# An attention and ELU-MLP kernel on one core: six-token runs for q and k of two batches, casting transfers for v, and reciprocals and batch 0 spread over other engines

## The chip, the cores and the metric

The kernel runs on one core of one Trainium2 chip. The core has five engines with instruction streams of their own: TensorE (PE in the profile, with its weight loads PEld), VectorE (DVE), ScalarE (ACT), GpSimd (POOL) and SyncE (SP), and 16 DMA engines that move data between the device's memory and the core's SBUF. Times are device microseconds of one execution; a kernel's time is the median of several.

## The reference, cut to what matters

```python
batch, n_heads, seq, head_dim = (8, 8, 576, 64)          # q, k, v in float32
# global part: q, k, v averaged over groups of 4 tokens, 144 of them, full softmax attention,
# each row of the result repeated 4 times
out_up = np.repeat(sm_attn(q_d, k_d, v_d), 4, axis=2)
# local part: softmax attention over |i - j| < 4
mask = np.abs(pos[:, None] - pos[None, :]) < 4
scores = np.where(mask, scale * np.matmul(q, k.transpose(0, 1, 3, 2)), -1000000000.0)
...
attn_out = out_up + out_local
# then a two-layer MLP on the 4608 tokens, 512 wide, 2048 hidden
x = attn_out.transpose(0, 2, 1, 3).reshape(4608, 512)
h = x @ w_in
g = np.where(h > 0.0, h, np.exp(np.minimum(h, 0.0)) - 1.0)
return g @ w_out
```

## The kernel before, in words

All matmuls run on fp16 operands; inputs and output are fp32.

**Attention.** The work goes by batch b (8 of them) and by pair j of heads (4 per batch). For each pair, `load` brings q, k and v as 96 tokens by (2 heads, 6 blocks, 64) into slots named `ld`. For most batches a token's row of 64 values is one run of 256 B. For the batches in `PAIRED` (0 and 1) q and k come as runs of two tokens, 512 B (L355). v comes with three tokens on either side of each block, the halos, which are transfers of their own of 3 partitions each (L366, L372, L375). All these are issued on SP's queue. `cast` turns them to fp16 (`c16`, `v16`): on DVE for q and k of batch 0, else on POOL (L409). `transposes` multiplies each block by an identity with averaging columns beside it, which gives the transposed q or k and its average over 4 tokens at once (L434 for paired batches, L440 for the others); ACT copies the results out of PSUM (L453, L462, L464). The averages of v come from another small matmul and a copy on DVE (L474, L483). `scores` does the local scores (96 queries by 102 keys) and the global ones (L499, L507), then two exps on ACT (L516) and a multiplication by the band's mask on DVE (L524).

**Denominators.** Once per batch, 76 small matmuls sum all exps (L544), and DVE takes reciprocals (L567). For batches 0 and 1 (`BY_PE`) PE spreads them over 128 partitions (L581), and ACT and DVE, in turn, copy them to `rcb` (L591). For the other batches they go to device memory (L596, rd<-rc) and come back in two broadcasting transfers (L602, rcb<-rd), all on ACT's queue.

**Outputs.** Per pair, PE computes local and global outputs (L626, L634), DVE multiplies by the reciprocals (L643, `xn`), and POOL adds local and global parts into the 512-token tiles `xt` of the MLP (L655).

**MLP.** Nine tiles of 512 tokens. mm1: 16 groups of 4 matmuls 128x512 against WI (L672), then exp on ACT (L678) and two operations on DVE (L680, L683) into `gt`. mm2: 4 groups of 16 matmuls against WO (L695), a copy on ACT (L710), a store on SP's queue (L713). WI and WO are cast while they are transferred, four transfers each, issued by POOL (L395).

**What sets the order.** A planner (`class Plan`) holds every operation with an engine, an assumed duration, a rank and the buffers it needs. It simulates all engines: each takes, whenever it is free, the ready operation of lowest rank whose buffers it can get. Transfers are modelled as one stream, with a rate in bytes per us for each kind and a depth beyond which SP issues no more. The order that comes out is emitted, and each engine then runs its own list strictly in that order. `PARAM` sets the ranks (how far attention of batch b leads tile b), `SLOTS` the buffers of each kind. `GATES` says which operation each of the eight weight transfers waits for, as (batch, pair, index of the cast). PSUM has eight banks; an attention operation takes two neighbouring banks or one, and shares them with the MLP.

Of the kernel before, what the change touches and what calls it, by code (L numbers as in the profile page):

```python
# [28 lines left out]
PAIRED = (0, 1)  # L29
BY_PE = (0, 1)  # L30
GATES = ((0, 2, 2), (0, 3, 0), (0, 3, 2), (0, 3, 2), (1, 1, 2), (1, 2, 2), (1, 3, 2), (1, 3, 2))


def _np_consts():
# [10 lines left out]
    by2 = np.zeros((QB, 48), dtype=np.float16)  # L45
    by2[np.arange(QB), np.arange(QB) // 2] = 0.25
    one = np.concatenate([eye, by4], axis=1)
    pair = np.concatenate([by2, eye, by2, np.zeros((QB, 96), dtype=np.float16)], axis=1)
# [10 lines left out]
    return m, one, pair, vr, ind, seed, sel.reshape(128, 640)  # L59
# [22 lines left out]
class Plan:  # L82
# [8 lines left out]
    def op(self, eng, dur, rank, fn, reads=(), writes=(), after=(), name="", nbytes=0, rate=1.0):  # L91
        o = Op(eng, dur, rank, fn, name)
        o.nbytes, o.rate = nbytes, rate
        for b in list(reads) + list(writes):
            o.pre.update(b.writers)
            if b not in o.bufs:
                o.bufs.append(b)
        o.pre.update(after)
        for b in writes:
            b.writers.append(o)  # L100
        for b in o.bufs:
            b.ops.append(o)
        self.ops.append(o)
        return o

    BANKS = ("two", "one", "hp", "op")

    def _take(self, b, free):
# [5 lines left out]
        banks = free["bank"]  # L114
# [29 lines left out]
    def run(self):  # L144
        free = {k: set(range(n)) for k, n in self.slots.items()}
        free["bank"] = set(range(8))
        self.count = {"hp": 0, "op": 0}
# [21 lines left out]
        events, now, dma, order = [], 0.0, 0.0, []  # L169
        n = 0  # L170
        while n < len(self.ops):
            for e, todo in ready.items():
                if busy[e] > now + 1e-9 or not todo or (e == "SP" and dma > now + self.depth):
                    continue
                todo.sort(key=lambda o: (o.rank, o.i))
                for o in todo:
                    got = []
# [11 lines left out]
                else:  # L189
                    continue  # L190
# [5 lines left out]
                if o.nbytes:  # L196
                    dma = max(dma, now + dur) + o.nbytes / o.rate
                    done = dma + 1.9
                    if e == "SP" and dma > now + self.depth:
                        heapq.heappush(events, (dma - self.depth, -1, None))  # L200
# [8 lines left out]
            now = events[0][0]  # L209
            while events and events[0][0] <= now + 1e-9:  # L210
                _, _, o = heapq.heappop(events)
                if o is None:
                    continue
                for q in o.post:
# [10 lines left out]
    def emit(self):  # L225
        for o in self.order:
# [4 lines left out]
    "ld": 9, "c16": 4, "v16": 8, "qt": 3, "kt": 3, "ex": 8, "vd": 8,  # L231
# [3 lines left out]
PARAM = dict(M0=43.0, P=36.0, LAG=0.8, LEAD=48.6, GAP=5.3, SC=2.7, DEN=28.0, OUT=9.0, OUTG=2.3, LOAD=22.6, warm=22.0,  # L235
             DEPTH=7.3, WI=-44.0, WO=14.0, WOG=6.0)
# [3 lines left out]
def kernel(  # L240
# [15 lines left out]
    def many(kind, shape, dt=FP16):  # L256
# [3 lines left out]
        "ld": many("ld", [KW, 2, NB, 64], FP32),  # L260
        "c16": many("c16", [QB, NB, 2, 64]),
        "v16": many("v16", [KW, NB, 2, 64]),
# [28 lines left out]
    plan.warm, plan.depth = PARAM["warm"], PARAM["DEPTH"]  # L291
# [3 lines left out]
    m_np, one_np, pair_np, vr_np, ind_np, seed_np, sel_np = _np_consts()  # L295
    C, cbuf = {}, {}

    def const(a, name, rank):
        t = sb.tile(list(a.shape), FP16, tag=name, name=name)
        src = nc.inline_tensor(a, name=name + "c").ap()  # L300
        C[name] = t
        return op("SP", 0.35, rank, lambda: nc.sync.dma_start(out=t[:], in_=src), name=name,
                  nbytes=a.size * 2, rate=150e3)

    c_pair = const(pair_np, "PAIR", -50)
    c_vr = const(vr_np, "VR", -48.5)
    c_mask = const(m_np, "MASK", -46.5)
    c_ind = const(ind_np, "IND", -44.5)
    c_seed = const(seed_np, "SEED", -44.4)
    c_sel = const(sel_np, "SEL", -40.5)  # L310
    c_one = const(one_np, "ONE", -35)
# [23 lines left out]
    def twos(src, b, j):  # L335
        a = src[b, 2 * j]
        return bass.AP(
            tensor=a.tensor, offset=a.offset,
            ap=[[2 * D, QB], [S * D, 2], [192 * D, 3], [1, 2 * D]],
        )  # L340
# [3 lines left out]
    def load(b, j):  # L344
        n = NPAIR * b + j
        r = -49.9 + 2 * j if b == 0 else late(b, j) - PARAM["LOAD"]
        bufs = []
        for i, (src, kind) in enumerate(((q, "ld"), (k, "ld"), (v, "ld"))):
            x = Buf(kind)

            def go(src=src, x=x, i=i):
                t = at(x)
                if i < 2 and b in PAIRED:
                    to = t[0:QB].rearrange("p e (c j) d -> p e c (j d)", c=3)
                    nc.sync.dma_start(out=to, in_=twos(src, b, j))  # L355
                elif i < 2:
                    nc.sync.dma_start(out=t[0:QB], in_=rows(src, b, j, 0, QB, 0, NB))
                else:
                    nc.sync.dma_start(out=t[3 : 3 + QB], in_=rows(src, b, j, 0, QB, 0, NB))  # L359
                    lo = 1 if n == 0 else 0  # L360
                    hi = NB - 1 if n == NPAIR * B - 1 else NB
                    if lo:
                        nc.gpsimd.memset(t[0:3, :, 0, :], 0.0)
                    if hi < NB:
                        nc.gpsimd.memset(t[96:KW, :, NB - 1, :], 0.0)
                        nc.sync.dma_start(  # L366
                            out=t[96:99, :, NB - 1, :], in_=rows(src, b, j, 93, 3, NB - 1, 1)[:, :, 0]
                        )
                    for c0, nblk, tok, p in ((lo, NB - lo, -3, 0), (0, hi, QB, 99)):
                        to, a = t[p : p + 3, :, c0 : c0 + nblk, :], rows(src, b, j, tok, 3, c0, nblk)  # L370
                        if nblk == NB:
                            nc.sync.dma_start(out=to, in_=a)  # L372
                        else:
                            for e in range(2):
                                nc.sync.dma_start(out=to[:, e], in_=a[:, e])  # L375

            rate = 290e3 if i < 2 and b in PAIRED else 185e3
            op("SP", 0.4 if i < 2 else 1.3, r + 0.01 * i, go, writes=[x], nbytes=96 * 768 * 4, rate=rate,
               name=f"load{b}{j}{'qkv'[i]}")
            bufs.append(x)  # L380
        st[b, j] = {"ld": bufs}

    wi_ops, wo_ops = {}, {}

    def weights(i):
        wi = i < 4
        if wi:
            src = moe_w_in.rearrange("(c p) m -> p c m", p=128)[:, :, 512 * i : 512 * i + 512]
            to, r = WI[:, :, 512 * i : 512 * i + 512], PARAM["WI"] + 0.1 * i
        else:  # L390
            n = 4 * (i - 4)
            src = moe_w_out.rearrange("(c p) m -> p c m", p=128)[:, n : n + 4, :]
            to, r = WO[:, n : n + 4, :], PARAM["WO"] + PARAM["WOG"] * (i - 4)
        b, j, x = GATES[i]
        o = op("POOL", 1.3, r, lambda: nc.gpsimd.dma_start(out=to, in_=src), name=f"w{i}", after=[st[b, j]["op"][x]],  # L395
               nbytes=128 * 8192, rate=320e3)
        (wi_ops if wi else wo_ops)[i % 4] = o

    def cast(b, j):
        s, r = st[b, j], late(b, j)  # L400
        s["c"], s["op"] = [], []
        for i, x in enumerate(s["ld"]):
            y = Buf("v16" if i == 2 else "c16")
            p = KW if i == 2 else QB
            eng = "DVE" if b == 0 and i < 2 else "POOL"

            def go(x=x, y=y, p=p, eng=eng):
                f = (nc.vector if eng == "DVE" else nc.gpsimd).tensor_copy
                f(out=at(y)[:], in_=at(x)[0:p].rearrange("p e c d -> p c e d"))  # L409

            s["op"].append(
                op(eng, 0.5 if eng == "DVE" else 0.85, r - 8 + i, go, reads=[x], writes=[y], name=f"cast{b}{j}{i}")
# [6 lines left out]
    def transposes(b, j):  # L419
        s, r = st[b, j], late(b, j)  # L420
        yq, yk, yv = s["c"]
        m = b in PAIRED
# [343 lines left out]
```

## Time and profile before

| | |
|---|---|
| median of 3 runs | 397.23 us (395.22 to 397.68) |
| the profiled execution's own time | 400.66 us |
| its span, first to last instruction | 398.6 us |
| granted TensorE clock, mean | 0.982 |
| busy: PE, DVE, ACT, POOL | 355.6, 231.7, 210.4, 130.6 us |
| DMA packets | 119716, 48.12 MB |
| first MoE matmul (L672) starts | 53.16 us |
| last MoE matmul (L695) ends | 394.9 us |

PE is TensorE's matmuls; their ends are modelled and neighbours overlap, so the distance from start to start says what one costs. A line such as "L409 POOL CAST v<-ld" gives the line of the code, the engine, the operation and the buffers. "SPq" is SP's DMA queue. A time in brackets is the idle time before an instruction, and the arrow names what ended it.

### The profile page before, as it was taken

How to read it: one execution, taken by the hardware profiler on the slowest of the kernel's cores; microseconds unless marked ns; L12 is line 12 of the kernel's file. 1: busy time of each engine (PE TensorE's matmuls, PEld its weight loads, DVE VectorE, ACT ScalarE, POOL GpSimd, SP SyncE). 2: the span in 40 equal slices, each digit the busy share in tenths (PEclk: the TensorE clock that was granted, in tenths of full speed). 3: DMA queues.
4: the chain of work that ended last, by engine and by line, in shares of the span. 5: the costliest groups of instructions: out<-in, count | busy, mean ns of one | idle time of the engine just before them, and what ended most of it. 6: DMA issues, size and time to landing. Idle time of an engine off the chain costs nothing.

```text
span 398.6 us, 8777 instructions
## 1 busy us (share of the span) xinstructions
PE 355.6 (89%) x3536; PEld 191.8 (48%) x3536; DVE 231.7 (58%) x404; ACT 210.4 (53%) x353; POOL 130.6 (33%) x207
## 2 busy tenths in 40 slices
PE   3741798999998399979999999989999999999996
PEld 2531654556554245545555545544555454444442
DVE  1430648766786237754868665857676666564530
ACT  3650376565974066635765756475749334444421
POOL 1333466039703472236127603570350023000000
PEclk9999998999999789989999999999999999999999
DMA  9999999958239997956449729701300221001012
GB/s 184 199 210 170 216 172 146 197 122 185 54 73 209 196 225 148 183 104 150 116 93 196 181 87 181 132 35 53 102 27 28 68 66 53 28 26 54 27 53 79
DMA packets 119716, 48.12 MB, mean 121 GB/s; under 512 B 98359, under 2 KB 115069, under 8 KB 119677
## 3 DMA queue, kind: packets, MB, share of 16 engines
q1 hardware_dynamic: 111325, 38.74, 44.5%
q0 software_dynamic: 4224, 4.19, 6.6%
q10 hardware_dynamic: 4128, 4.65, 5.3%
q8 instruction: 27, 0.44, 0.5%
q14 instruction: 12, 0.10, 0.1%
HBM read 42.11 MB, written 9.66 MB: 130 GB/s over the span
## 4 chain that ended last, share of the span: by engine, by line
PE 75%; DMA 10%; SPq 7%; DVE 3%; issue 2%; ACT 2%; POOL 2%; ACTq 0%; POOLq 0%; DVEq 0%
PE bank L695 29%; PE bank L672 29%; DMA ld<-in_v_dram 5%; DMA rcb<-rd 4%; SPq L372 4%; PE bank L440 3%; PE bank L499 3%; PE bank L626 2%; PE bank L544 2%; PE bank L474 2%; SPq L359 2%; PE bank L434 1%; DVE e L680 1%; POOL v L409 1%; PE bank L507 1%
## 5 line engine op out<-in xcount | busy, mean ns | idle before, releaser
L672 PE MATMUL bank<-xt,WI 128*128 128x512 f16 x576 | 146.3, 384 | 3.3 <-DVE gt L683 1.8
L695 PE MATMUL bank<-WO,gt 128*128 128x512 f16 x576 | 146.5, 384 | 0.0
L678 ACT ACTIVATE e<-bank 128x512 f16<-128x512 f32 x144 | 85.8, 599 | 86.8 <-PE bank L672 69.3
L680 DVE TENSOR_SCALAR e<-e 128x512 f16<-128x512 f16 x144 | 56.4, 393 | 81.3 <-ACT e L678 80.9
L683 DVE SCALAR_TENSOR_TENSOR gt<-bank,e 128x512 f16<-128x512 f32 x144 | 98.8, 688 | 5.0
L672 PEld LDWEIGHTS <-WI 128*128 128x128 f16 x576 | 53.7, 98 | 63.6 <-issue 6.9
L695 PEld LDWEIGHTS <-gt 128*128 128x128 f16 x576 | 53.2, 99 | 57.0 <-issue 2.2
L409 POOL CAST c<-ld 96x768 f16<-96x768 f32 x56 | 48.0, 866 | 91.2 <-PE bank L440 47.2
L655 POOL TENSOR_TENSOR xt<-xn 128x288 f16<-128x288 f16 (+8 forms) x96 | 49.1, 538 | 45.4 <-DVE xn L643 45.3
L516 ACT ACTIVATE ex<-bank 102x864 f16<-102x864 f32 x64 | 55.6, 889 | 14.0 <-PE bank L507 13.8
L409 POOL CAST v<-ld 102x768 f16<-102x768 f32 x32 | 28.8, 901 | 61.4 <-DMA ld<-in_v_dram 40.3
L643 DVE TENSOR_TENSOR xn<-bank,rcb 128x720 f16<-128x720 f32 x32 | 28.3, 903 | 18.7 <-POOL xt L655 7.9
L710 ACT COPY os<-bank 128x512 f32<-128x512 f32 x36 | 21.2, 588 | 33.1 <-PE bank L695 25.4
L524 DVE TENSOR_TENSOR ex<-ex,MASK 102x1152 f16<-102x1152 f16 x32 | 28.7, 898 | 14.1 <-ACT ex L516 14.1
L474 PE MATMUL bank<-v,VR 102*72 102x128 f16 x192 | 18.5, 240 | 18.2 <-POOL v L409 16.0
L440 PE MATMUL bank<-ONE,c 96*128 96x120 f16 x288 | 22.3, 217 | 6.2 <-DVE xn L643 6.2
L440 PEld LDWEIGHTS <-c 96*128 96x128 f16 x288 | 19.1, 98 | 15.6 <-issue 6.5
L453 ACT CAST qt<-bank 128x720 f16<-128x720 f32 x24 | 18.2, 758 | 15.5 <-PE bank L440 14.8
L474 PEld LDWEIGHTS <-VR 102*72 102x72 f16 x192 | 14.9, 126 | 22.8 <-issue 15.6
L462 ACT CAST kt<-bank 128x576 f16<-128x576 f32 x32 | 22.1, 689 | 6.5 <-PE bank L440 4.9
L483 DVE CAST vd<-bank 72x256 f16<-72x256 f32 x32 | 13.2, 413 | 17.6 <-PE bank L474 17.4
L499 PEld LDWEIGHTS <-kt 64*102 64x102 f16 x384 | 13.5, 138 | 17.3 <-issue 9.6
(34 smaller groups left out, 176.3 us busy)
## 6 DMA issues: line engine op xcount, KB each, us to landing
ld<-in_q_dram SPq DMA_DIRECT2D x32, 288.0 KB
ld<-in_k_dram SPq DMA_DIRECT2D x32, 288.0 KB
ld<-in_v_dram SPq DMA_DIRECT2D x32, 288.0 KB
out_dram<-os SPq DMA_DIRECT2D x36, 256.0 KB
rcb<-rd ACTq DMA_DIRECT2D x12, 360.0 KB
WI<-in_moe_w_in_dram POOLq DMA_DIRECT2D x4, 512.0 KB, 9.8
WO<-in_moe_w_out_dram POOLq DMA_DIRECT2D x4, 512.0 KB, 6.8
ld<-in_v_dram SPq DMA_DIRECT2D x62, 9.0 KB
```

Of the source, the lines that this page charges most:

```text
L409: f(out=at(y)[:], in_=at(x)[0:p].rearrange("p e c d -> p c e d"))
L440: nc.tensor.matmul(o, t[:, c, :, :], C["ONE"][:], start=True, stop=True)
L474: nc.tensor.matmul(one(z, 0, 72, 128 * (c // 3), 128 * (c // 3) + 128), C["VR"][:, 48 - 24 * (c % 3) : 120 - 24 * (c % 3)], t[:, c, :, :], ...
L516: lambda e=e: nc.scalar.activation(out=at(x)[:, e], in_=two(sc[e], 0, KW, 0, HB + SD), func=AF.Exp, scale=SCALE),
L524: nc.vector.tensor_tensor(out=a, in0=a, in1=mk, op=AB.mult)
L643: lambda: nc.vector.tensor_tensor(out=at(w)[:], in0=two(z, 0, 128, 0, GW), in1=at(y)[:, j], op=AB.mult),
L655: nc.gpsimd.tensor_tensor(out=at(xt(t))[:, j, o : o + n - a], in0=ln, in1=gn, op=AB.add)
L672: nc.tensor.matmul(one(h, 0, 128, 0, TBLK), WI[:, dc, 128 * fc : 128 * fc + 128], at(x)[:, dc, :], start=(dc == 0), stop=(dc == DMC - 1),)
L678: op("ACT", 0.55, r, lambda: nc.scalar.activation(out=at(e)[:], in_=one(h, 0, 128, 0, TBLK), func=AF.Exp), reads=[h], writes=[e], name=f"e ...
L680: op("DVE", 0.36, r, lambda: nc.vector.tensor_scalar(out=at(e)[:], in0=at(e)[:], scalar1=1.0, scalar2=-1.0, op0=AB.min, op1=AB.add), reads ...
L683: op("DVE", 0.69, r, lambda: nc.vector.scalar_tensor_tensor(out=at(gt)[:, fc, :], in0=one(h, 0, 128, 0, TBLK), scalar=0.0, op0=AB.max, in1 ...
L695: nc.tensor.matmul(one(z, 0, 128, 0, DM), at(gt)[:, fc, 128 * tt : 128 * tt + 128], WO[:, fc, :], start=(fc == 0), stop=(fc == FCN - 1),)
```

## The change

It consists of these parts:

- q and k of batches 0 and 1 (`SIX`) are loaded in runs of six tokens, 1536 B, in place of two. Their averages over 4 tokens now come from six accumulating matmuls of 144 columns beside six of 96.
- v is no longer loaded per pair on SP's queue and cast on POOL. Per batch, `load_v` issues four transfers on POOL's queue that cast on the way into one of two large `v16` buffers: two halos of 3 partitions and two halves of 96 partitions.
- The seven constants become two transfers: CA (identity, averaging matrices) ahead of all loads, CB (mask, sums, spreads).
- WI goes in five transfers, the first two of 256 columns, and all weights wait for other casts than before (`WIC`, `GATES`).
- In batch 0 the cast of k moves from DVE to POOL, its copies out of PSUM from ACT to DVE; denominators are taken in two groups of two pairs; the spreads' copies are all on ACT; some of POOL's adds go to DVE.
- The reciprocals' way through device memory is issued on POOL's queue in place of ACT's.
- While the planner's clock is below 36 us, it puts small matmuls on zeros (128x128 by 128 columns, into bank 7) wherever PE would have nothing to do.
- Only batch 0 may use all pairs of banks (`EARLY`). The planner's model of the transfers and the ranks in `PARAM` have other values, and parts of some buffers (`PARTS`) no longer wait for one another's writers.

```diff
-PAIRED = (0, 1)
+SIX = (0, 1)
+EARLY = 1
+DEN_GROUPS = {0: ((0, 1), (2, 3))}
 BY_PE = (0, 1)
-GATES = ((0, 2, 2), (0, 3, 0), (0, 3, 2), (0, 3, 2), (1, 1, 2), (1, 2, 2), (1, 3, 2), (1, 3, 2))
+WIC = (0, 256, 512, 1024, 1536, 2048)
+GATES = ((0, 3, 0), (0, 3, 1), (0, 3, 1), (1, 1, 1), (1, 1, 1), (1, 2, 0), (1, 2, 1), (1, 3, 0), (1, 3, 1))
...
+            if b in reads or b.kind not in self.PARTS:
+                o.pre.update(b.writers)
...
+    PARTS = ("v16", "rcb", "xt", "gt", "ex")
...
+                    if e == "PE" and now < self.fill and self.zero.i < 0:
+                        o = Op("PE", 0.107, 0, self.filler, "fill")
...
-    "ld": 9, "c16": 4, "v16": 8, "qt": 3, "kt": 3, "ex": 8, "vd": 8,
+    "ld": 9, "c16": 4, "v16": 2, "qt": 3, "kt": 3, "ex": 8, "vd": 8,
...
-PARAM = dict(M0=43.0, P=36.0, LAG=0.8, LEAD=48.6, GAP=5.3, SC=2.7, DEN=28.0, OUT=9.0, OUTG=2.3, LOAD=22.6, warm=22.0,
-             DEPTH=7.3, WI=-44.0, WO=14.0, WOG=6.0)
+PARAM = dict(M0=43.0, P=36.0, LAG=0.84, LEAD=48.6, GAP=6.2, SC=2.7, DEN=29.4, OUT=8.8, OUTG=1.0, TV=18.4, LOAD=11.5,
+             VLOAD=3.4, warm=3.4, FILL=36.0, DEPTH=8.9, WI=-44.0, WO=43.8, WOG=2.5)
...
+    def fill():
+        nc.tensor.matmul(PS[:, 7, 384:512], zero[:, 0:128], zero[:, 128:256], start=True, stop=True)
...
+    c_a = consts((("ONE", one_np), ("BY6", by6_np), ("VR", vr_np)), "CA", -60)
+    m2_np = m_np.reshape(KW, NB * QB)
+    c_b = consts((("MASK", m2_np), ("IND", ind_np), ("SEED", seed_np), ("SEL", sel_np)), "CB", -47.5)
...
+    def sixes(src, b, j):
         a = src[b, 2 * j]
+        return bass.AP(tensor=a.tensor, offset=a.offset, ap=[[NB * D, QB], [S * D, 2], [1, NB * D]])
...
+    def load_v(b):
+        x = Buf("v16")
+        r = late(b, 3) - PARAM["VLOAD"] if b else -46.0
+        pre = [st[0, 0]["op"][1]] if b == 0 else []
+        a = v[b, 0]
+
+        def main(h):
+            t = at(x)[3 : 3 + QB].rearrange("p j e c d -> p (j e c) d")
+            nc.gpsimd.dma_start(
+                out=t[:, 24 * h : 24 * h + 24, :],
+                in_=bass.AP(tensor=a.tensor, offset=a.offset + 24 * h * QB * D, ap=[[D, QB], [QB * D, 24], [1, D]]),
+            )
...
-            eng = "DVE" if b == 0 and i < 2 else "POOL"
+            eng = "DVE" if b == 0 and i == 0 else "POOL"
...
                 for c in range(NB):
                     if m:
+                        nc.tensor.matmul(
+                            PS[:, z.slot[0] + 1, HB : HB + SD], t[:, c, :, :], C["BY6"][:, SD * c : SD * c + SD],
+                            start=(c == 0), stop=(c == NB - 1),
+                        )
+                        if c < 3:
+                            natural(c)
...
+            eng = "DVE" if b == 0 and which == "k" else "ACT"
...
-            op("ACT", 0.15, r + 1, lambda: nc.scalar.dma_start(out=at(d)[:], in_=at(c)[:]),
+            op("POOL", 0.8, r + 1, lambda: nc.gpsimd.dma_start(out=at(d)[:], in_=at(c)[:]),
                reads=[c], writes=[d], name=f"spo{b}").lag = 3.0
...
+                op("POOL", 0.8, r + 1.1, lambda e=e: spread(e), reads=[d], writes=[y], name=f"spi{b}{e}").lag = 4.0
...
+            eng = "DVE" if b == 0 and g == 1 and t == 0 else "POOL"
...
+        load_v(b)
+        for j in range(NPAIR):
+            pool_v(b, j)
+        for js in DEN_GROUPS.get(b, (range(NPAIR),)):
+            denominators(b, js)
```

## The prediction, as it was put on record before the result was known

> **What bounds the kernel now.** I read the busy shares first, then the span in stretches, then the chain that ended last, then the timeline around its stalls. The page:
>
> ```profile
> PE 355.6 (89%) x3536; PEld 191.8 (48%) x3536; DVE 231.7 (58%) x404; ACT 210.4 (53%) x353; POOL 130.6 (33%) x207
> ...
> q1 hardware_dynamic: 111325, 38.74, 44.5%
> q0 software_dynamic: 4224, 4.19, 6.6%
> ```
>
> TensorE is the engine to count against, but its 89% is an average. The stretches show where it is not filled (columns: stretch, its length, busy us of PE, PEld, DVE, ACT, POOL with counts, granted clock, share of the DMA engines, GB/s):
>
> ```profile
> 0.00:53.00 53.00, 27.97 (x362) 21.50 (x362) 15.46 (x24) 20.63 (x35) 18.28 (x41) 1.00 1.04 195
> 53.00:72.00 19.00, 16.98 (x130) 9.27 (x131) 13.73 (x22) 14.47 (x27) 9.94 (x13) 0.91 0.98 167
> 72.00:113.00 41.00, 41.00 (x546) 22.73 (x544) 30.35 (x48) 27.15 (x47) 21.29 (x29) 1.00 0.60 122
> 113.00:140.00 27.00, 19.00 (x203) 10.58 (x200) 14.35 (x28) 10.37 (x17) 7.42 (x11) 0.91 0.92 180
> ...
> 160.00:178.00 18.00, 15.03 (x150) 8.32 (x149) 11.63 (x23) 9.43 (x16) 6.70 (x10) 0.95 0.81 157
> 178.00:398.60 220.60, 215.62 (x1951) 109.36 (x1949) 135.16 (x242) 115.35 (x194) 56.60 (x89) 1.00 0.33 83
> ```
>
> See two things: until 72 us the DMA engines are full and PE is not, and from 178 us it is the other way round. The chain says which transfer the first stretch ends on, and the timeline of PE when the MoE begins:
>
> ```profile
> 22.19 7.67 SPq L372
> 29.91 7.60 DMA ld<-in_v_dram
> 37.56 0.83 POOL v L409
> 38.44 0.80 PE bank L474 x6
> 39.23 1.83 PE bank L544 x58
> ```
> ```profile
> 53.16 1.86 PE L672 MATMUL bank<-xt,WI 128*128 128x512 f16 x4 [0.21 <-ACT qt L464]
> ```
>
> The last v of batch 0 lands at 37.5 us: SP's queue was held 7.67 us at a halo of it, while WI's four transfers, let go at 17.7 and 23.0 us, shared the engines. Everything else of batch 0 was done by 28.3. The stall at 113 to 140 is POOL's order:
>
> ```profile
> 135.18 0.83 POOL L409 CAST v<-ld 102x768 f16<-102x768 f32 x1 [5.58 <-DMA ld<-in_v_dram]
> ...
> 135.97 3.39 POOL L655 TENSOR_TENSOR xt<-xn 128x288 f16<-128x288 f16 x6
> ...
> 137.45 0.91 DVE L643 TENSOR_TENSOR xn<-bank,rcb 128x720 f16<-128x720 f32 x1 [7.62 <-POOL xt L655]
> ...
> 138.42 0.76 PE L440 MATMUL bank<-ONE,c 96*128 96x120 f16 x6 [6.19 <-DVE xn L643]
> ```
>
> A cast waits for v; the adds stand behind it on POOL, xn's buffers behind those, PE last.
>
> **The sum for before.** Full-speed prices from 178 to 220 us, start to start: four 128x512 matmuls 0.865 us, six transposes 0.32, pooling of v 0.35, scores 0.54, outputs 0.51, denominators 1.06. The 1152 MoE matmuls are 249.2; seven batches at 4 x (2 x 0.32 + 0.35 + 0.54 + 0.51) + 1.06 = 9.2 make 64.6, the costlier transposes and spreads of batch 1 some 2: 315.6 after the first MoE matmul. PE's last ends at 394.9. Subtracting the same prices times the counts of each stretch leaves the lost time: 5.4 in 53 to 72, 1.2 to 113, 9.1 to 140, 0.9 to 160, 4.1 to 178, 5.7 later: 26.4. So 53.2 + 315.6 + 26.4 + 3.7 of tail = 398.9 against 398.6 of span; the execution's own time is 400.66, 2.1 more, and 3.4 above the median 397.23.
>
> **The change, part by part.**
>
> *q, k of batches 0 and 1.* 9216 packets of 512 B become 3072 of 1536 B. Rows: two such loads ended DVE's waits at 4.65 and 5.70, so 295 KB in 1.05 us, 281 GB/s. WI and WO: 8.39 MB of source in 6.6% of 16 x 398.6 engine-us, 319 GB/s. The 4.72 MB save between 0 and 2.0 us of DMA; I take 1.5, nearer the long runs. The transposes keep their number per pair (12 each, 240 columns per block in all), so PE is even within 0.1 us.
>
> *v.* Off SP: 99 issues and their waits. Off POOL: 32 casts, 28.8 us. Onto POOL: 32 issues, 16 of 2304 packets or so and 16 of about 144. The weights' issues (512 packets) took 742 to 903 ns. If that is flat, 32 x 0.78 = 25 us; if it goes by packets, 16 x 3.4 + 16 x 0.78 = 67. With k's casts and the reciprocals (below) POOL stands at 144 to 186 us of some 365: not the bound either way. Queued behind an issue that waits for one of the two v buffers are casts and adds; the buffer's last reader is the batch two earlier, so I put that wait at 0. The upper end is what v's casts waited for the same readers, 21.0 us in 8 times.
> The packets: q1's mean is 44.5% x 16 x 398.6 / 111325 = 25.5 ns. A cast of 256 B to 128 B is not in the trace: half of 25.5 below, the 2 KB casting packet of q0 (6.6% of the same / 4096 = 103 ns) above. I take 25.5, the row with the same bytes read. That is 4896 x 25.5 / 16 = 7.8 us a batch.
>
> *Constants.* Seven issues of 0.28 to 0.46 become two. The first, 283 KB, stands ahead of the first q where 54 KB stood: 229 KB at 281 GB/s, 0.8 us later.
>
> *Batch 0.* Per pair ACT loses k's evictions (0.81 + 0.28), DVE gains them; k's cast goes from DVE (0.56) to POOL (0.82). ACT had 4.0 us a pair, then has 2.9; DVE has 0.56 + 1.1 + 0.76 + 0.42 = 2.8: even, and under the loads' pace. All four spreads' evictions on ACT: 2 x 0.76 more, hidden beside DVE's xn (0.90 each). DVE's adds (four, bound 0.4 to 0.9) replace POOL's: POOL's 12 adds had taken 5.7 us.
>
> *WI behind pair 3's casts instead of pair 2's v.* This is the largest term. Ahead of it stand 2.36 MB of q, k (8.4 us at 281), 0.37 MB of constants (1.3) and v (7.8). From a first q at 5.45, that is 5.45 - 1.05 + 17.5 = 21.9 for all, k of pair 3 at about 19. Its chain: cast 0.82, transposes 0.66, evictions 1.09, scores 0.75, two exps 1.78, mask 0.76, six handoffs near 0.1: 25.5. Then half the denominators 0.6, reciprocal 1.06, spread 0.35, two evictions 1.5, last xn 0.9, add 0.73 with handoffs: 31. Over 0 to 60 us q1 took 75.4% of 16 x 60 for 24917 packets, 29 ns, so the loads run a little longer: 33. Low end 28 (loads at 319). High end: batch 0, WI and constants, 6.4 MB as written, at the 195 GB/s of the first row is 33, plus 11 of chain: 44.
>
> *Fill matmuls.* Pooling one v took 0.85 us at 14 to 24 us and 0.50 from 200, with a granted clock of 1.00 in both; six paired transposes 1.14 at 10 to 22 and 0.66 at 58; four MoE matmuls 1.86 at 53.2 and 1.03 later. Without the fill the chain above would pay 0.5 (transposes), 0.3, 0.6 and the first MoE group 0.9: some 2 us, held in the 33. The fills are on PE alone and planned into its idle time; a fill ahead of late data costs at most its own 0.1 us.
> The Trainium skill, TensorE: Matmul & The Clock Gate, Part 1, says that activity releases a throttled default clock after some 3.4 us and an idle window of that length restores it. The durations agree; the granted clock does not show it. By that rule T0 without fills would be 35.
>
> *Reciprocals on POOL.* 18 issues of 0.33 to 0.66 leave ACT, 18 of about 0.78 (14 us) come to POOL. The second and third wait for rd to land: 2.3 us (112.3 to 114.6) and 3.2 (158.7 to 161.9) in before, when they held ACT. On POOL adds and casts queue behind: 0 to 3.2 x 6 = 19 us; xn must wait for that to count, and outputs rank 20 us behind the denominators, so I take 2 in all. They also stand behind v on one queue: 7.8 us of that 20.
>
> *Lost time after T0.* 53 to 72 was cold PE and loads: 5.4 kept, since some 10 MB of source are still to come then (batch 1 3.6, WO 4.2, half of WI 2.1). 113 to 140: v's cast is gone, 9.1 to 2 (cover gone: late q, k casts). 160 to 178, where xn waited 2.63 for rcb: 4.1 to 1.5. The rest 7.8 to 6, the reciprocals' 2 among it. Sum 15, low end 8, high end 27 (no gain).
>
> Sum: 33 + 315.6 + 15 + 3.7 + 2.1 = 369.4 against 400.66; less the 3.4 by which that lay above the median, 366.
>
> **Rivals.**
>
> *A, the DMA engines stay the bound until batch 1 and WO are in.* By packets that phase is about 2 us shorter than the 70 us of before (WO landed about then). PE could start at 33 and then lack WO and batch 1. For it: shares of 0.98 to 1.04 until 72. Against: between 33 and 68 there are 13.8 us of first-layer matmuls and 11 of batch 1 to do without WO, which fill 25 of the 35. If half of the 20 us is waited out again, 366 + 10, and with 5 more for POOL's waits on rd and buffers, 381. The Trainium skill, DMA: Bandwidth & Descriptors, section Issuing engines are not separate DMA queues, says that transfers of all issuers share 16 engines and another issuer saves only issue time. The share of 1.04 agrees.
>
> *B, slower: the casting packet.* 39168 of them. Beside them stand per batch q, k 9216 x 25.5 / 16 = 14.7 us, rcb 5.3% of 398.6 / 6 = 3.5, stores of 1.05 MB at 319 GB/s 3.3. The last batch must be in some 70 us before the end, so by 325 for 398.6. There the engines' work is 3 to start, 2.2 constants, 14.8 q and k of batches 0 and 1, 26.3 weights (6.6% of 398.6) and 6 x 21.5, 175 in all, plus 39168 p / 16. The same count for before (batches 0 and 1, weights, constants) gives 63 us for what had landed by 70 (WO's last issue at 63, 6.8 to land), so 0.9. At 0.9 x 325 = 292 it decides at p = (292 - 175) x 16 / 39168 = 48 ns. At 55 ns the end is 7 x 39168 / 16 / 0.9 = 19 us later: some 415. For it: 103 ns for the 2 KB cast. Against: that row reads eight times the bytes.
>
> *C, all stalls go.* T0 29, lost 8: 29 + 315.6 + 8 + 3.7 + 2.1 - 3.4 = 355. For it: after 178 us PE lost only 5.7 in 217 with the DMA share at 0.33. Against: WO and batch 1 still come late.
>
> **How the numbers follow.** Forecast 0.50 (360 to 374), A 0.23 (374 to 390), C 0.14 (350 to 360), B 0.10 (over 397), no effect (within 1%) 0.03. The predicted time is the forecast's, 366. Leaving out B, no effect and the outer part of A and C gives 353 to 386. A measurement of this kernel tells about 1% from no change: faster 0.87, same 0.03, slower 0.10.
>
> **What would show it.** First MoE matmul near 33; no DMA wait above 3 us ahead of denominators of batch 0; no POOL wait on v; a v packet on q0 near 25 ns; PE full from about 70. Wrong if q0's mean is over 48 ns, if PE has a gap of over 5 us between 33 and 70 (A), or if POOL's waits before L655 end on rd.

## The result and the profile after

The changed kernel takes 376.65 us in the median of four runs (374.11 to 382.67), beside 397.46 for the kernel before on the same chip: a ratio of 0.9459, with an interval of 0.9386 to 0.9533. (382.67 ran at a lower clock and does not enter the ratio.) The forecast was 366 with 360 to 374 of its own; the time lies 10.7 above it, inside the whole range of 353 to 386 but in the interval that was given to rival A. The profiled execution took 376.44 with a span of 374.5, so it stands at the median, where that of before stood 3.4 above its own.

The page of the kernel after, busy times and the two large DMA queues:

```profile
PE 357.9 (96%) x3815; PEld 202.1 (54%) x3815; DVE 228.1 (61%) x410; ACT 205.6 (55%) x349; POOL 146.9 (39%) x226
...
q0 software_dynamic: 55920, 13.90, 35.4%
q1 hardware_dynamic: 64864, 28.97, 32.5%
```

The work of v has gone from q1 to q0, and POOL does more in all, at the low end of the 144 to 186 us that were forecast. The share of 96% for PE holds fills too: of the 279 more matmuls than before, 183 are fills on zeros, and 96 come from the averages of batches 0 and 1, which now take 12 matmuls for each q or k in place of 6. So the stretches have to say where the time came from (columns as in the prediction):

```profile
0.00:43.20 43.20, 34.87 (x588) 30.79 (x589) 18.37 (x31) 15.87 (x26) 23.05 (x43) 0.84 1.20 210
...
53.00:72.00 19.00, 17.83 (x269) 10.98 (x269) 15.24 (x30) 15.64 (x27) 8.87 (x11) 1.00 1.59 179
...
113.00:140.00 27.00, 25.61 (x302) 14.42 (x304) 16.42 (x27) 16.35 (x29) 16.53 (x24) 1.00 1.11 174
...
160.00:178.00 18.00, 18.00 (x222) 9.91 (x217) 13.50 (x26) 14.54 (x25) 11.07 (x14) 1.00 1.26 177
178.00:374.50 196.50, 191.68 (x1690) 97.22 (x1687) 117.61 (x216) 100.57 (x170) 53.73 (x88) 1.00 0.35 72
```

Two gains are seen. From 113 to 140 us PE idled 8.0 us before (27.00 less 19.00) and 1.4 now; from 160 to 178 it idled 3.0 and now not at all. And the MoE begins at 43.1 in place of 53.2. Before that, the chain of waits of the kernel after names one transfer:

```profile
12.65 17.97 DMA v<-in_v_dram
30.67 1.44 PE bank L539 x12
```

PE's timeline shows the wait, and the first MoE matmul:

```profile
30.67 1.44 PE L539 MATMUL bank<-v,CA 102*72 102x128 f16 x12 [3.70 <-DMA v<-in_v_dram]
...
43.09 1.03 PE L740 MATMUL bank<-xt,WI 128*128 128x512 f16 x4
```

The second half of batch 0's v, 0.59 MB of source, is issued at 12.65 and takes 18 us to land. WI does not look like the cause: POOL issues it from 18.5 us on, behind v on the same queue, and in the first experiment below v is in by 20.3 although WI is issued from 15.0 on. What is new beside v is on SP's queue: batch 1's q and k, whose long runs SP issues from 6.9 to 20.1 us. To 31 us the engines moved 6.95 MB as written, and batch 0 with the constants is 3.64 of it.

After v another 12.4 us pass to the MoE. The groups of PE between 30.6 and 43.1 us say what fills them:

```profile
L320 PE MATMUL bank<-zero 128*128 128x128 f16 x39 | 4.5, 269 | 0.0
L690 PE MATMUL bank<-ex,v 102*64 102x96 f16 x48 | 2.8, 282 | 0.0
```

The costliest group are 39 fills on zeros, 4.5 us of busy time and 3.8 from start to start: idle slots in the planner's model, but in the run data came late and the fills stood in line between the outputs and the MoE.

### The profile page after: what moved, and what is told of

Same layout as the page of the kernel before. It is cut to its first block, busy times and chain, and to the rows that moved or that the text cites. A ratio compares the mean times of both kernels' runs of the same rounds, so it can differ in the third digit from the quotient of the medians.

```text
span 374.5 us, 9192 instructions
## 1 busy us (share of the span) xinstructions
PE 357.9 (96%) x3815; PEld 202.1 (54%) x3815; DVE 228.1 (61%) x410; ACT 205.6 (55%) x349; POOL 146.9 (39%) x226
## 3 DMA queue, kind: packets, MB, share of 16 engines
q0 software_dynamic: 55920, 13.90, 35.4%
## 4 chain that ended last, share of the span: by engine, by line
PE 78%; DMA 12%; DVE 3%; POOL 2%; issue 2%; ACT 2%; SPq 0%; DVEq 0%; ACTq 0%
PE bank L740 30%; PE bank L763 29%; DMA rcb<-rd 5%; DMA v<-in_v_dram 5%; PE bank L497 4%; PE bank L690 3%; PE bank L539 3%; PE bank L564 3%; PE bank L610 2%; DMA ld<-in_k_dram 1%; DVE xn L707 1%; DVE e L748 1%; PE bank L698 1%; PE bank L320 1%; POOL c L462 1%
## 5 line engine op out<-in xcount | busy, mean ns | idle before, releaser
L462 POOL CAST c<-ld 96x768 f16<-96x768 f32 x60 | 52.9, 896 | 47.6 <-issue 30.3
L723 POOL TENSOR_TENSOR xt<-xn 128x288 f16<-128x288 f16 (+8 forms) x92 | 45.0, 517 | 57.2 <-DVE xn L707 57.0
L581 ACT ACTIVATE ex<-bank 102x864 f16<-102x864 f32 x64 | 53.4, 888 | 16.0 <-PE bank L572 15.8
L589 DVE TENSOR_TENSOR ex<-ex,CB 102x1152 f16<-102x1152 f16 x32 | 24.6, 770 | 34.2 <-ACT ex L581 34.2
L778 ACT COPY os<-bank 128x512 f32<-128x512 f32 x36 | 21.2, 588 | 30.6 <-PE bank L763 29.0
L497 PEld LDWEIGHTS <-c 96*128 96x128 f16 x288 | 19.5, 97 | 10.7 <-issue 0.4
L512 ACT CAST qt<-bank 128x720 f16<-128x720 f32 x24 | 18.2, 759 | 10.1 <-PE bank L497 7.7
L497 PE MATMUL bank<-CA,c 96*128 96x120 f16 x288 | 23.0, 215 | 0.5 <-DVE xn L707 0.5
L660 POOL DMA_DIRECT2D rd<-rc x6 | 3.6, 608 | 41.1 <-DVE rc L633 41.1
L539 PE MATMUL bank<-v,CA 102*72 102x128 f16 x192 | 15.9, 225 | 3.9 <-DMA v<-in_v_dram 3.7
L405 POOL DMA_DIRECT2D v<-in_v_dram x16 | 19.3, 1209 | 0.0
L320 PE MATMUL bank<-zero 128*128 128x128 f16 x183 | 16.3, 244 | 2.6 <-DVE rc L633 1.6
L523 ACT CAST kt<-bank 128x576 f16<-128x576 f32 x24 | 15.4, 642 | 5.6 <-PE bank L497 4.7
```

The costliest lines, as they stand in the source:

```text
L462: f(out=at(y)[:], in_=at(x)[:].rearrange("p e c d -> p c e d"))
L497: nc.tensor.matmul(o, t[:, c, :, :], C["ONE"], start=True, stop=True)
L539: nc.tensor.matmul(one(z, 0, 72, 128 * (c // 3), 128 * (c // 3) + 128), C["VR"][:, 48 - 24 * (c % 3) : 120 - 24 * (c % 3)], t[:, j, :, c, ...
L581: lambda e=e: nc.scalar.activation(out=at(x)[:, e], in_=two(sc[e], 0, KW, 0, HB + SD), func=AF.Exp, scale=SCALE),
L589: nc.vector.tensor_tensor(out=a, in0=a, in1=mk, op=AB.mult)
L723: (nc.vector if eng == "DVE" else nc.gpsimd).tensor_tensor(out=at(xt(t))[:, j, o : o + n - a], in0=ln, in1=gn, op=AB.add)
```

## The experiments

Each kernel is the changed one with the edit that is shown, except for `e11_packets`, which only moves data. The start of the MoE and "lost" are those of the profiled execution; the median is that of four executions (of ten for `e12_v_on_sp`). "Lost" is the end of PE's last matmul, less the start of the first MoE matmul, less the 315.6 us of work of the prediction's sum: 26.1 in before, 12.0 in after. Kernels with the same number in the first column ran on one chip, with the kernel before beside them; across chips the ratios are compared.

| chip | kernel | median us | ratio to before, interval | first MoE matmul | lost |
|---|---|---|---|---|---|
| 7 | e1_hold_b1 | 382.49 | 0.9569, 0.9505 to 0.9633 | 41.1 | 21.4 |
| 7 | e2_b1_short | 378.92 | 0.9444, 0.9353 to 0.9535 | 34.1 | 23.5 |
| 7 | e3_v_first | 391.49 | 0.9810, 0.9766 to 0.9854 | 56.1 | 14.4 |
| 7 | e4_no_fill | 372.72 | 0.9347, 0.9305 to 0.9390 | 40.1 | 11.5 |
| 2 | c0_after_again | 376.50 | 0.9441, 0.9368 to 0.9514 | 42.1 | 13.7 |
| 2 | e5_rec_act | 379.37 | 0.9531, 0.9479 to 0.9584 | 40.5 | 15.9 |
| 2 | e8_no_qk1 | 367.15 | 0.9218, 0.9160 to 0.9277 | 36.5 | 10.2 |
| 2 | e9_nofill_rec_act | 372.59 | 0.9349, 0.9255 to 0.9443 | 38.1 | 11.8 |
| 1 | e10_no_six | 381.94 | 0.9548, 0.9478 to 0.9619 | 36.6 | 25.8 |
| 1 | e12_v_on_sp | 399.50 | 0.9985, 0.9950 to 1.0020 | 54.6 | 21.5 |
| 1 | e13_hold_same_order | 374.07 | 0.9318, 0.9232 to 0.9405 | 37.3 | 11.4 |

**Batch 1's loads held until batch 0's v is in.**

```diff
+                if first:    # b == 1, j == 0, q
+                    nc.sync.dma_start(out=seen[:], in_=at(st[0])[3:4, :, 0, 0, 0:16])
                 nc.sync.dma_start(...)
...
+               after=vms if b == 1 and j == 0 else ())    # vms: the issues of v's two halves of batch 0
```

> Edit: SP's first load of batch 1 waits until v of batch 0 has landed (SP reads a few values of it first). In the changed kernel v's second half was issued at 12.65 us and landed at 30.6, and the first MoE matmul started at 43.1, where 33 was predicted. Theory share: the long runs of q and k of batch 1 on SP's queue take the engines from v's short casting packets. Then v lands near 22 and the MoE starts near 35; the end gains some 4 to 7 us, less what batch 1's later arrival gives back. Theory price: a casting packet of v itself costs about 38 ns (the mean of q0), so v lands at 26 or later and the MoE starts at 39 or later; the end gains 0 to 3 us.

SP read batch 0's v at 20.25 us and PE pooled it at 21.59 without a wait, so it had landed some ten us earlier: the part of the theory that long runs of batch 1 slow v is borne out. But the added dependence made the planner write another order, with batch 1's v ahead of the MoE. PE's timeline of this kernel:

```profile
21.59 1.50 PE L545 MATMUL bank<-v,CA 102*72 102x128 f16 x24
...
39.83 1.50 PE L545 MATMUL bank<-v,CA 102*72 102x128 f16 x12 [4.70 <-DMA v<-in_v_dram]
```

The second line is batch 1's pooling, 4.7 us of waiting just ahead of the MoE at 41.1; behind the start 21.4 us are lost, and the kernel is slower, 382.49, where both theories had it faster or the same. On what a start is worth the run says nothing.

**Batch 1 in runs of one token.**

```diff
-SIX = (0, 1)
+SIX = (0,)
```

> Edit: q and k of batch 1 in runs of one token (256 B), batch 0 still in runs of six. Theory share, if engines are shared packet by packet: v then stands against packets of its own length, gets half in place of a seventh, lands near 24, the MoE starts near 37; later loads lose about 5 us of engine time, so the end is within 3 us of 376. If they are shared by bytes, or by theory price: v lands no earlier than 30, the MoE starts at 43 or later, and the end is 0 to 5 us later.

v was pooled at 26.95 without a wait and the MoE began nine us earlier than in after, as by the theory of shares, yet the time is no shorter. The gain was given back between 53 and 90 us. DVE's timeline of this kernel, and after it the stretches:

```profile
58.79 1.06 DVE L633 RECIPROCAL rc<-bank 128x144 f16<-128x144 f32 x1 [0.29 <-PE bank L610]
...
81.27 2.55 DVE L707 TENSOR_TENSOR xn<-bank,rcb 128x720 f16<-128x720 f32 x3 [0.19 <-PE bank L698]
```
```profile
53.00:66.00 13.00, 11.04 (x142) 6.40 (x137) 7.52 (x14) 3.85 (x6) 4.53 (x5) 0.74 1.45 182
...
80.00:90.00 10.00, 6.46 (x125) 5.49 (x122) 4.12 (x7) 4.01 (x6) 7.74 (x15) 0.66 0.52 120
```

Batch 1's reciprocals are ready at 58.8, 6.3 us before those of after (65.06), so its q and k were not late. Its outputs come at 81.3, after's at 72.4: the planner, with another estimate of the loads, put 56 matmuls with WO between, 36 of them in one row. From 53 to 66 PE idles 2.0 us at a granted clock of 0.74, from 80 to 90 3.5 us at 0.66. No engine waits for a transfer between 36 and 95 us. So this run does not price the start; it prices another order.

**v issued first.**

```diff
-        pre = [st[0, 0]["op"][1]] if b == 0 else []
+        pre = []
```

> Edit: the transfers of v of batch 0 no longer wait for the first cast of k; POOL issues them from about 1 us on. Theory share: v then stands beside batch 0's own long runs from the start and lands with them near 20; the MoE starts at 34 to 37; the end gains 4 to 8 us. Theory price: v lands near 24 at best, q and k of batch 0 are later by up to 4, the MoE starts at 38 to 41, and the end gains 2 to 4.

A miss for both. The halos are issued from 1.7 us on and the halves from 3.3, and still v lands only at 26.3; PE, whose order now has v's pooling ahead of the scores of two pairs, waits. Its timeline:

```profile
26.43 2.84 PE L539 MATMUL bank<-v,CA 102*72 102x128 f16 x24 [9.92 <-DMA v<-in_v_dram]
```

The rest of batch 0 stands behind that wait, and the MoE starts at 56.1. Issued early, v took 23 us to land, not less than the 18 of after.

**No fills.**

```diff
-             VLOAD=3.4, warm=3.4, FILL=36.0, DEPTH=8.9, WI=-44.0, WO=43.8, WOG=2.5)
+             VLOAD=3.4, warm=3.4, FILL=0.0, DEPTH=8.9, WI=-44.0, WO=43.8, WOG=2.5)
```

> Edit: no fill matmuls. The prediction put them at 2 us before the first MoE matmul. If v's landing at 30.6 decides, the work ahead of it has slack, and what PE does after it was slow even with fills (granted clock 0.57 from 31 to 43.2), so theory share says 0 to 2 us later. Rival: the fills carry the gain of the first stretch, then the MoE starts 4 us or more later and the end likewise.

The sign was wrong in both: without fills the kernel takes 372.72, and the MoE starts at 40.1. The first group of four MoE matmuls costs 1.89 us in place of 1.03, as expected, but from v's pooling to the MoE it is 10.0 us (30.16 to 40.13), less than the 12.4 of after, although both halves are pooled in that time. PE is at its slow rate in both: 12 matmuls of the outputs take 0.69 us, where they take 0.45 at full rate. So the fills behind v, 3.8 us from start to start, bought no speed there. PE does not wait for v here; its denominators, at the slow rate, come as late.

**The changed kernel once more, and the reciprocals back on ACT.** The first of the two is the changed kernel without an edit.

> The changed kernel as it is, a second time, to stand beside the three others on one chip. 376.65 us was its median; 374 to 379.

376.50: this chip gives the same time as the first.

```diff
-            op("POOL", 0.8, r + 1, lambda: nc.gpsimd.dma_start(out=at(d)[:], in_=at(c)[:]),
+            op("ACT", 0.15, r + 1, lambda: nc.scalar.dma_start(out=at(d)[:], in_=at(c)[:]),
...
-                nc.gpsimd.dma_start(
+                nc.scalar.dma_start(
```

> Edit: the reciprocals' way through device memory is issued on ACT's queue again (18 issues), all else as changed. The prediction charged the move to POOL with 2 us. In the changed kernel xn waited 4.1 us for rcb in 3 places and rcb took 6.4 to 6.9 us to land behind v and the casts' loads. Theory: a queue of its own lets it land earlier, 1 to 3 us gained. Rival: rcb's time is that of the shared engines, and ACT's issues hold its exps, then 0 to 2 us lost.

379.37 beside 376.50, with intervals that overlap: POOL's queue costs the reciprocals nothing that can be seen. xn waited 7.9 us in 3 times for rcb on this route, and on POOL's 4.1 in 3 (after) and 5.7 in 3 (the repeat); the loss of 2 us that the prediction took for the move is not there.

**Without batch 1's q and k.** This kernel leaves out the loads of batch 1's q and k, 2.36 MB; the casts read what batch 0 left in the buffers, so batch 1's result is not the attention's.

```diff
-            op("SP", 0.45, r + 0.01 * i, go, writes=[x], ...)
+            if b != 1:
+                op("SP", 0.45, r + 0.01 * i, go, writes=[x], ...)
```

> Leaves out the loads of q and k of batch 1 (its casts read what batch 0 left in the slots): 2.36 MB less, some 8 us of engine time, of the first 70 us. Theory A, the transfers up to batch 1 and WO bound that stretch: the end comes 6 to 9 us earlier, wherever the MoE starts. Theory start, the late first MoE matmul is what cost the forecast its 10 us, and the stretch behind it is not bound: the MoE starts near 35 and the end moves by the same 8. Rival, neither: PE's own order after 43 us sets the end; then the end moves by less than 3 us.

367.15, 9.35 us shorter than the changed kernel. PE's timeline, v's pooling and the first MoE matmuls:

```profile
21.70 1.50 PE L540 MATMUL bank<-v,CA 102*72 102x128 f16 x24
...
36.46 1.90 PE L741 MATMUL bank<-xt,WI 128*128 128x512 f16 x8
```

v is pooled at 21.70 without a wait; the MoE starts 5.7 us earlier than in the repeat, and 3.4 us less are lost after it. Neither reading is excluded by this alone, since 2.36 MB are also some 8 us of the engines' time; but most of the gain passes through the start.

**No fills, and the reciprocals on ACT.** The edits of the two kernels together.

```diff
-             ... FILL=36.0, ...
+             ... FILL=0.0, ...
...
-            op("POOL", 0.8, r + 1, lambda: nc.gpsimd.dma_start(out=at(d)[:], in_=at(c)[:]),
+            op("ACT", 0.15, r + 1, lambda: nc.scalar.dma_start(out=at(d)[:], in_=at(c)[:]),
```

> Edit: no fill matmuls, and the reciprocals on ACT's queue. Without the fills alone 372.7 us was measured. If the two add, 370 to 372; if the reciprocals' queue makes no difference, 372 to 374; above 374 if ACT's issues cost.

372.59, as without fills alone: the reciprocals' route shows no price. The kernel beside it on the same chip, with the reciprocals on ACT and with fills, took 379.37, and the two intervals lie apart (0.9255 to 0.9443, and 0.9479 to 0.9584): without fills the kernel is faster. This is not the price of the fills alone, since the planner kept bank 7 for them and writes another order without them.

**No batch in runs of six.**

```diff
-SIX = (0, 1)
+SIX = ()
```

> Edit: q and k of batches 0 and 1 in runs of one token (256 B), no runs of six; all else as changed. 18432 short packets in place of 3072 long ones: at 25.5 ns against 75, some 15 us of engine time more in the first 70 us. Theory A (transfers up to batch 1 and WO are the bound): the end comes 10 to 15 us later, 386 to 392. Theory start: only batch 0's half counts, 380 to 385. If short packets cost less beside v than alone, 376 to 380.

381.94, by the ratios some 4 us above the repeat, which ran on another chip, with intervals that overlap by 0.004 (0.9548, 0.9478 to 0.9619, beside 0.9441, 0.9368 to 0.9514). That is where the theory of the start had it, but not for its reason: the start is again early, 36.6, with v pooled at 28.07; the loss is in the 90 us behind. Here batch 1's reciprocals come at 73.6, 8.6 later than in after. No engine waits for a transfer between 36 and 95 us, but the planner rewrote the order here too, so what the short runs cost stays open. The 75 ns that the expectation takes for a long packet are what the planner's rate of 330 GB/s gives; the next kernel measures 97.

**Transfers alone.** This kernel computes nothing of the reference. It times six stages of transfers, one behind the other: casting halves of v alone (2304 packets of 256 B to 128 B each), the same without a cast from SP, loads of q in runs of six (192 packets of 1536 B each), casting halves beside such loads of k, casting halves beside loads of single tokens (1152 packets of 256 B each), and these alone. A tiny instruction on DVE marks each landing.

```diff
+    casts(0, 8)
+    seen(V)
...
+    casts(4, 4)
+    sixes(k, 0, 16)
+    seen(V[:4] + L)
...
+    casts(6, 4)
+    ones(q, 4, 16)
+    seen(V[:4] + L)
```

> Computes nothing of the reference: it transfers in stages that wait for one another. Stage 1: 8 casting halves of v from POOL; 2: the same shapes uncast from SP; 3: 16 loads in runs of six from SP; 4: 4 casting halves beside 16 six-token loads; 5: 4 casting halves beside 16 one-token loads; 6: 16 one-token loads alone. The prediction's price of a casting packet was 25.5 ns, the deciding one 48. Theory share by packets: in stage 4 v lands after the long loads, in stage 5 before or with the short ones; by bytes: the other way round.

The timeline of this kernel, one or more lines of each stage, in brackets what DVE waited for each landing (with its own 0.15 us that is the time between two landings):

```profile
14.69 0.15 DVE L62 TENSOR_TENSOR tok<-tok,v 1x1 f32<-1x1 f32 x1 [1.72 <-DMA v<-in_v_dram]
16.57 0.15 DVE L62 TENSOR_TENSOR tok<-tok,v 1x1 f32<-1x1 f32 x1 [1.74 <-DMA v<-in_v_dram]
...
37.34 0.15 DVE L62 TENSOR_TENSOR tok<-tok,f 1x1 f32<-1x1 f32 x1 [2.74 <-DMA f<-in_v_dram]
...
54.05 0.15 DVE L62 TENSOR_TENSOR tok<-tok,l 1x1 f32<-1x1 f32 x1 [1.01 <-DMA l<-in_q_dram]
...
67.39 4.65 POOL L78 DMA_DIRECT2D v<-in_v_dram  x4 [56.67 <-DVE l L56]
80.28 0.15 DVE L62 TENSOR_TENSOR tok<-tok,v 1x1 f32<-1x1 f32 x1 [12.15 <-DMA v<-in_v_dram]
91.04 0.15 DVE L62 TENSOR_TENSOR tok<-tok,v 1x1 f32<-1x1 f32 x1 [10.62 <-DMA v<-in_v_dram]
92.90 0.15 DVE L62 TENSOR_TENSOR tok<-tok,v 1x1 f32<-1x1 f32 x1 [1.71 <-DMA v<-in_v_dram]
...
94.95 2.87 DVE L62 TENSOR_TENSOR tok<-tok,l 1x1 f32<-1x1 f32 x16
...
110.72 0.15 DVE L62 TENSOR_TENSOR tok<-tok,v 1x1 f32<-1x1 f32 x1 [3.85 <-DMA v<-in_v_dram]
115.71 0.15 DVE L62 TENSOR_TENSOR tok<-tok,v 1x1 f32<-1x1 f32 x1 [4.85 <-DMA v<-in_v_dram]
...
142.37 0.15 DVE L62 TENSOR_TENSOR tok<-tok,l 1x1 f32<-1x1 f32 x1 [1.24 <-DMA l<-in_k_dram]
```

Alone, a half lands every 1.88 us: 1.88 x 16 / 2304 = 13.0 ns for a casting packet on each of the 16 engines. Without the cast it is 2.88 us, 20.0 ns. A long load came each 1.16 us in the middle of its stage, 97 ns for each of its packets, and a load of single tokens each 1.39, 19.3 ns. Beside long runs the first half lands 12.9 us after its issue and the second 10.8 later; the next two come at the speed of a half alone, and none of the sixteen long loads has to be waited for any more.
On each engine a half is 2304 / 16 = 144 packets. If the engines took one packet of each queue in turn, a half would need 144 x (13 + 97) = 15.8 us beside long runs, and 144 x (13 + 19.3) = 4.7 beside single tokens. If they shared by bytes, 24 long packets would go by for the 144, and the half would need 4.2 us. Beside single tokens the halves come 4.0 to 5.0 us apart. Beside long runs the second half's 10.8 us leave (10.8 - 1.9) / 0.097 = 92 long packets for its 144; the first half's 12.9, less the 3.3 us that a first half takes in stage 1 beyond its own 1.9, leave some 80. These are estimates, but they lie far from 24: the share goes by packets, about one long one for 1.7 short ones, and not by bytes.
The Trainium skill, DMA: Bandwidth & Descriptors, section Queues, rings and completion order, says that an engine goes round the queues it has work for and drains a whole packet, some 9 to 17 descriptors, from one before it goes to the next. The stages agree with queues that take turns; a packet of the profile is one run here, so how much a turn holds they do not show.

**v on SP's queue, cast on POOL.** One fp32 buffer per batch, loaded by SP, and four casts on POOL.

```diff
-            nc.gpsimd.dma_start(
+            nc.sync.dma_start(
...
+        for j in range(NPAIR):
+            op("POOL", 0.85, r + 0.3 + 0.1 * j,
+               lambda j=j: nc.gpsimd.tensor_copy(out=at(y)[:, j], in_=at(x)[:, j]), reads=[x], writes=[y], name=f"vc{b}{j}")
```

> Edit: v per batch as changed, but issued on SP's queue in fp32 into one buffer and cast on POOL, four casts a batch. If the casting transfers are what the gain after the first MoE matmul rests on (no cast on POOL that waits for v, with the adds behind it), the end comes 6 to 15 us later, 382 to 392. If the gain rests on the order of the loads and of the weights, the end stays within 3 us of 376.5.

399.50, later than either expectation: the whole gain is gone. The waits of this kernel:

```profile
POOL v L434 <- DMA v<-in_v_dram: 24.1, 3, 16.2
...
PE bank L543 <- POOL v L434: 12.9, 2, 10.0
```

The cast on POOL waits 16.2 us once, PE 10.0 behind it, and the MoE starts at 54.6, where it started before the change. The buffer is a single one and the order is a new one: SP issued the halves of batch 0 at 19.7 and 34.9 us, behind batch 1's loads, where POOL had issued them at 9.7 and 12.7. So the run shows that v's way decides over the gain; how much of it is the queue, the cast, the buffer or the order stays open.

**Held, in the same order.** No fills, and the wait of the first experiment, but with the engines' orders as in the kernel without fills; only batch 1's loads move, behind v's issue.

```diff
+        i = [o.name for o in self.order].index("vm01")
+        held = [o for o in self.order[:i] if o.name.startswith("load1")]
+        for o in [o for o in self.order[: i + 1] if o not in held] + held + self.order[i + 1 :]:
```

> Edit: no fill matmuls, and SP's loads of batch 1 wait until v of batch 0 has landed, with the order of each engine's work left as it is without fills (372.7 us, first MoE matmul at 40.1). Both theories: v lands near 22, the MoE starts at 34 to 37. Theory A: the same bytes have to come before WO and batch 1, so the end moves by less than 2 us. Theory start: the end comes 3 to 6 us earlier, 367 to 370.

PE's timeline without fills, and then with the hold as well: first MoE matmul, first matmul with WO:

```profile
40.13 1.89 PE L740 MATMUL bank<-xt,WI 128*128 128x512 f16 x4
...
59.43 1.03 PE L763 MATMUL bank<-WO,gt 128*128 128x512 f16 x4
```
```profile
37.32 0.59 PE L745 MATMUL bank<-xt,WI 128*128 128x512 f16 x2
...
56.68 1.03 PE L768 MATMUL bank<-WO,gt 128*128 128x512 f16 x4
```

In the profiled executions all is shifted alike, by 2.8 us at both places and by 3.0 at the end (372.81 and 369.78), with the same loss behind the start, 11.5 and 11.4. With the order kept, an earlier start was passed on whole. The earlier start is not that of v, though: v was in by 18.7 here, when SP read it, but in both kernels PE pools it without a wait, behind its denominators (at 29.37, and at 30.16 without the hold). 2.0 of the 2.8 us come behind that, where PE was at its full rate from about 33 us on and without the hold from about 42. The medians do not confirm the gain: 374.07 (369.78 to 377.02) beside 372.72. What holding batch 1 is worth stays open within some 3 us.

## Why the prediction was right and wrong

*The direction and most of the mechanism were right.* v's halo no longer holds SP, and POOL's cast no longer holds the adds, xn's buffers and PE at 135 us. With the start and the lost time as measured the sum is 43.1 + 315.6 + 12.0 + 3.7 + 2.0 = 376.4, the profiled execution's own time; it must be, since the lost time is what is left over. From 366 that is 10.1 for the start, 3.0 less of lost time, and 3.4 because the profile of after did not lie above its median as that of before did. The 3.0 less lie mostly ahead of 72 us: the prediction's prices times the counts of each stretch, an estimate, leave some 2.6 us lost there, where 5.4 were kept for a cold PE and loads. They leave 1.8 at 113 to 140, where 2 was said, and nothing at 160 to 178, where 1.5 was.

*The step that failed is the start of the MoE,* 33 forecast and 43.1 measured, just inside its high end of 44. It was summed up from 2.36 MB of q and k, 0.37 MB of constants and v: 21.9 us for all to be in. That is a sum of what is ahead in the order of issue, at the full rate of the engines. v is on another queue than q and k, and SP runs on to batch 1 beside it; v then takes turns with long packets. Its last half was in at 30.6, 8.7 us late; with batch 1 held or left out it was in by 20.3 and 21.7, as summed. PE waited 3.70 us for it and then went on at its slow rate. But not all of the ten us are v's. Where PE did not wait for v, the MoE started at 34.1 (batch 1 in short runs), 36.5 (batch 1 left out), 37.3 (held in the same order) and 40.1 (no fills). From 43.1 to the first two, which have fills, v's landing and the slow rate behind it explain 6.6 to 9.0. In the rest the forecast's chain behind k of pair 3 was too short: it ends on one xn and one add, 1.6 us, where with batch 1 left out four xn and DVE's adds took from 30.55 to 36.4. How the ten us divide is argued across kernels of different orders, and not shown.

*The fills were taken at a gain of 2 us,* with 0.1 for one that is ahead of late data. 39 of them stood in the chain behind v, 3.8 us from start to start. Two kernels without them took 372.7 and 372.6, beside 376.5 and 376.65; these intervals overlap by at most 0.008. With the reciprocals on ACT in both, on one chip, the intervals lie apart (372.59 and 379.37). So a gain by leaving them out is shown on that route, with the order that the planner then writes; its size, 4 to 7 us by the kernel it is taken from, is not.

*Rival A gave the right time by luck, for a reason that the traces do not show.* It wanted PE to start early and then lack WO and batch 1. After 43.1 PE does not idle more than 0.8 us at a time until 95, no engine waits for a transfer between 36 and 95, and the lost time is 12.0, within the 8 to 27 and below the 15 of the forecast. Batch 1's transfers did bound, but ahead of the MoE and by way of v. The two kernels that started early and ended no earlier had other orders; the one with the order kept passed the start on.

*Rival B fell.* A casting packet costs 13.0 ns alone, the low end, where 25.5 was taken and 48 was the point of decision. The mean of q0, named as its sign, came to 37.9 ns in after (35.4% of 16 x 374.5 us for 55920 packets): it holds the time beside other queues and the weights' longer packets, so it is no price of a casting packet. *The reciprocals on POOL* were put at 2 us and cost nothing measurable, though POOL waited 6.7 us in 4 times for rd. *POOL's issues* of a half took 1.18 to 1.34 us in after, those of 512 packets 0.75: neither flat nor by packets, and 146.9 us of POOL in all. *The stall at 113 to 140* went as forecast, to 1.4 us of idle time where 2 was said. *Runs of six* were put at 1.5 us of DMA time; without them the kernel took some 4 longer, not clear of the noise, and how much of it by order is open. The transposes did not keep their number, 12 matmuls for each q or k in place of 6, but their price is even as said: 0.64 us from start to start at 43.95, where six took 0.66 at 58 before.

## What to carry to other kernels

A late transfer shares the engines with all that other queues have under way, so its landing is the time of what runs beside it as well as of what is ahead; short packets beside long ones get the smaller part of the bytes. Work that only fills gaps belongs where the gap is in the run, not where a planner's clock has it: behind late data it stands in the chain. And where a planner writes the order, undoing one part gives another order too: read the trace before calling a difference the price of that part, and keep the order fixed where a few us are to be told apart.

## What the runs showed of the hardware that was not expected

- A packet of 256 B that is cast to 128 B took 13.0 ns on an engine, the same packet without the cast 20.0. The first were issued on POOL's queue and the second on SP's, so whether the cast or the queue makes the difference is open.
- The granted clock is not a record of PE's rate at the start. The same 24 matmuls of v's pooling took 2.77 us without fills (at 30.16) and 1.50 with them (at 26.95, batch 1 short), and the stretch around both shows 1.00. The mean clock of 0.999 without fills beside 0.977 with them does not mean a faster PE in the first 40 us.
- The last fill ahead of v ended at 26.1 us, and PE idled for v from 27.0 to 30.7. The granted clock was 1.00 to 26.6, and 0.57 from 30.7 to 43.1: the rate that PE had was lost in one wait of 3.7 us.
